# The final threshold search of an attention and expert kernel: comparisons against key differences, a written plan of fill-in work, and constants made ahead

## The chip, the cores and the metric

The kernel runs on one NeuronCore of one Trainium2 chip. The metric is device time in microseconds (us): the whole program once, from start to end; the median of several runs counts.

The engines have short names below. PE is TensorE (matrix products), PEld its weight loads, DVE is VectorE, ACT is ScalarE, POOL is GpSimd, SP is SyncE, which issues most DMA transfers. Each engine works its own instructions strictly in the order in which the program issues them.

## The reference

```
x = attention(q, kv, w_sr):                      # 4 batches, 12288 queries, 128 channels
    k = v = mean4x4(kv) @ w_sr                   # 768 keys and values per batch
    s = (q @ k.T) / sqrt(128)
    a = exp(s - max(s)); a /= sum(a) + 1e-9
    x = a @ v
for each batch b:                                # capacity = 128
    scores = x[b] @ w_gate                       # one score per row, 12288 of them
    top = the 128 rows with the largest score
    ye = relu(x[b, top] @ w1) @ w2               # w1 128x1024, w2 1024x128
    out[b] = x[b]; out[b, top] += sigmoid(scores[top]) * ye
```

## The kernel before

The work is cut into 192 blocks of 256 queries, 48 for each of the four batches, run in one loop (`for i in range(nb)`, nb = 192). One turn of the loop takes scores of block i+1 (`S`, PE into one of two PSUM buffers `s_buf`, shown as tiles `s`), the row maximum of block i (`s_max`, DVE), its exponentials (`exp`, ACT), their split in two 16-bit halves and transposes by DMA (`turn`, SP), and, `LAG` = 5 turns later, the product with the values (`AV`, 2 x 18 matmuls on PE into the PSUM tile `o_two`). From that product DVE takes the reciprocal `rz` of the row sum (`sums`, `recip`), the gate score of each row (tile `sc`) and the scaled output rows (`finish`, tile `x`); every fourth block SP stores an `x` tile of 512 KB. The tile `x` has two buffers.

Each batch then needs its 128 best rows. For batches 0 to 2 this (`topk`, `pick`) is a generator, kept in the list `select`, of which the loop takes one piece per turn; it is advanced by `advance(select)`. Its last piece of the third batch, the expert product of the 128 rows it picked (gather of the rows into `xe`, `xt`, the products with `w1` into `hs`, with `w2`, and a scatter into `out`) is still open when the loop ends.

After the loop comes the tail, which this change rewrites. Five blocks, 187 to 191 (`tail`), still lack their product, and the last batch its search:

1. Gate scores of the last two blocks are not taken from their products but from the exponentials, four DVE instructions of 768 columns into `kv_sum` (`gsum`).
2. `AV` of blocks 187 to 189, 30 filler matmuls (`warm`, products of ones that nobody reads), then `put` for each: scores and, on ACT because `ended` is set, the scaled rows `x`. `key_part` turns scores into sortable integers (`key`), whose upper 16 bits are `high` and lower 16 `low`.
3. `find` searches the 16-bit threshold digit by digit, two bits at a time, eight steps; it runs once on `high`, then on `rest` (the low halves of those that tie). In a step three thresholds are tested: DVE compares the 96 columns with a threshold and sums the hits (`junk`, `cnt3`), for two thresholds or three; where ACT is free it takes the third with a sign function (a "shared" step). PE sums the counts over the partitions with a matrix of ones into `counts` (tile `s`), DVE compares these with the need (`hit`, its sum is `dig`), and makes the next thresholds `tv` from `dig` and `base3`.
4. In every step `fill()` issues one piece of other work: in the first three a piece of `select`, then a piece of `later()` (half of an `AV` of 18 matmuls, or a `put` of blocks 190 and 191) and beside it a piece of `select` as long as that is not one for PE; when `later` is done, `select` alone.
5. `pick` makes row numbers from the threshold, gathers the rows (`xe`), runs what is left of `select`, 12 filler matmuls, then the expert product of the last batch and its scatter, the last transfer of the program.

The step in `fill` and the start of a step in the chain of `find` read, before:

```
if len(steps) > 3 and next(rows, True) is None:
    if select and select[0][1] != "pe":
        advance(select)
else:
    advance(select)
...
dve.scalar_tensor_tensor(out=tv, in0=dig.broadcast_to([P, 3]), scalar=float(1 << sh), in1=base3, op0=ALU.mult, op1=ALU.add)
```

Every engine call goes through one helper, so that all rows of the profile carry its line, L54; the tile names tell the instructions apart.

Of the kernel before, what the change touches and what calls it, by code (L numbers as in the profile page):

```python
# [19 lines left out]
P = 128  # L20
# [48 lines left out]
def attention_topk_mlp(ctx, tc, a, outs, capacity):  # L69
# [432 lines left out]
    def sums(n):  # L502
        b, blk = blocks[n]
        o, sg = st[n]["o"], kvset[b]["sg"]
        rz = sm.tile([P, QT], F32, name="rz")
        r = dve.tensor_scalar(out=rz, in0=o[:, :, C], scalar1=1e-9, scalar2=sg[:, 3:4], op0=ALU.add, op1=ALU.mult)
        st[n]["rz"] = rz
        st[n]["reads"] = [r.ins]
# [6 lines left out]

    def finish(n):
        b, blk = blocks[n]
        o, rz = st[n]["o"], st[n]["rz"]
        if blk % GROUP == 0:
            xt_[b] = ob.tile([P, GROUP * QT, C], F32, name="x")  # L520
        x = xt_[b]
        if b not in scores:
            scores[b] = tk.tile([P, NCOL], F32, name="sc")
        rows = x[:, (blk % GROUP) * QT:(blk % GROUP + 1) * QT]
        r = []
        if not direct(n):
            r.append(dve.tensor_tensor(out=scores[b][:, blk * QT:(blk + 1) * QT], in0=o[:, :, C + 1], in1=rz, op=ALU.mult))
        if ended:
            r += scaled(rows, o, rz)
        else:  # L530
            r.append(dve.tensor_tensor(out=rows, in0=o[:, :, 0:C], in1=rz.rearrange("p (j o) -> p j o", o=1).broadcast_to([P, QT, C]), op=ALU.mult))
# [5 lines left out]
        st[n].setdefault("reads", []).extend(y.ins for y in r)  # L537
# [53 lines left out]
    def pick(b, mask):  # L591
# [32 lines left out]
        for j0 in range(0, capacity, P):  # L624
# [125 lines left out]
    spare = [s_buf[i][:, 2 * k:2 * k + 2].rearrange("p k q -> p (k q)")[:, 0:QT * VC].rearrange("p (j c) -> p j c", j=QT) for i, k in ((0, 0), (1, 1), (1, 2))]  # L750
    gates = s_flat[0][:, BANK:BANK + M]
    tail = list(range(nb - LAG, nb))
    dest = dict(zip(tail, (spare[0], o_all, spare[1], spare[2], o_all)))
    whole = sm.tile([P, 2 * QT], F32, name="whole")

    def search_constants():
        jt = tk.tile([P, 3], F32, name="jt")
        for j in range(3):
            pool.memset(jt[:, j:j + 1], float(j + 1))
        half16 = tk.tile([P, P], BF16, name="half16")  # L760
        pool.memset(half16, -0.5)
        mid16 = tk.tile([P, 1], BF16, name="mid16")
        pool.memset(mid16, NCOL / 2.0)
        tv0 = tk.tile([P, 3], F32, name="tv0")
        dve.tensor_scalar(out=tv0, in0=jt, scalar1=float(1 << 14), scalar2=-0.5, op0=ALU.mult, op1=ALU.add)
        return jt, half16, mid16, tv0

    for i in range(nb):
# [4 lines left out]
        if i == nb - NBLK // 2:  # L773
            jt, half16, mid16, tv0 = search_constants()
# [6 lines left out]
        if i == nb - 1:  # L781
            room["select"] = lot
        s_max(i)
        if old:
            AV(m, 0)
# [40 lines left out]
        if i == nb - 1:  # L826
            for k in range(KT):
                pe.transpose(gates[:, k * P:(k + 1) * P], kvset[b]["raw"][:, k, 2 * P:].broadcast_to([P, P]), ident)
            AV(tail[0], 0, spare[0])
# [7 lines left out]
        if i == nb - 1:  # L837
            AV(tail[0], 1, spare[0])
        if old:
            sums(m)  # L840
            recip(m)
            finish(m)
# [24 lines left out]
    sc = scores[b]  # L867
    key = tk.tile([P, NCOL], I32, name="key")
    high, low, eqh, rest = (tk.tile([P, NCOL], U16, name=x) for x in ("high", "low", "eqh", "rest16"))
    junk = tk.tile([P, 3, NCOL], BF16, name="junk16")  # L870

    def put(m):
        if not direct(m):
            sums(m)
            recip(m)
        finish(m)
        return st[m]["reads"]

    def key_part(lo, hi):
        k, x = key[:, lo:hi], sc[:, lo:hi].bitcast(I32)  # L880
        dve.tensor_scalar(out=k, in0=x, scalar1=31, scalar2=-(1 << 31), op0=ALU.arith_shift_right, op1=ALU.bitwise_or)
        dve.tensor_tensor(out=k, in0=k, in1=x, op=ALU.bitwise_xor)
        dve.tensor_copy(high[:, lo:hi], k.bitcast(U16).rearrange("p (n h) -> p n h", h=2)[:, :, 1])

    part = kvu.tile([P, P, TAPS // 2], F32, name="kv_sum").rearrange("p k t -> p (k t)")[:, 0:M]
    gsum = sm.tile([P, 2 * QT], F32, name="gsum")
    for k in range(2 * QT):
        r = dve.scalar_tensor_tensor(out=part, in0=st[nb - 2 + k // QT]["a"][:, k % QT * M:(k % QT + 1) * M], scalar=1.0, in1=gates, op0=ALU.mult, op1=ALU.mult, accum_out=gsum[:, k:k + 1])
        others(r, st[tail[0]]["av"])
# [3 lines left out]
    dve.tensor_tensor(out=sc[:, NCOL - 2 * QT:], in0=gsum, in1=share, op=ALU.mult)  # L893
# [3 lines left out]
    for m in tail[1:3]:  # L897
        for j in range(QT):
            AV(m, j, dest[m])
    warm(30, s_flat[1][:, 0:P])  # L900
    put(tail[0])
    put(tail[1])
    key_part(0, NCOL - 3 * QT)
    put(tail[2])
    key_part(NCOL - 3 * QT, NCOL)

    def later():
        for m in tail[3:]:
# [3 lines left out]
            put(m)  # L912

    rows = later()
    steps = []
# [11 lines left out]
    def find(x, need, name, then=None):  # L927
        tv = tv0
        lo = tk.tile([P, 1], F32, name=name)
        pool.memset(lo, -0.5)  # L930
        shared = True
        for sh in range(14, -1, -2):
            cnt = tk.tile([P, 3], BF16, name="cnt3")
            n = 2 if shared else 3
            if shared:
                with nc.allow_low_precision(reason="whole numbers up to 96"):
                    act.activation(junk[:, 2], x, AF.Sign, bias=tv[:, 2:3], scale=-1.0, accum_out=cnt[:, 2:3])
                pe.matmul(counts[:, 2:3], ones16, mid16, start=True, stop=False)
                pe.matmul(counts[:, 2:3], half16, cnt[:, 2:3], start=False, stop=True)
            for j in range(n):  # L940
                dve.tensor_scalar(out=junk[:, j], in0=x, scalar1=tv[:, j:j + 1], scalar2=None, op0=ALU.is_ge, op1=ALU.add, accum_out=cnt[:, j:j + 1])
            if sh < 14:
                dve.scalar_tensor_tensor(out=lo, in0=dig, scalar=float(1 << sh + 2), in1=lo, op0=ALU.mult, op1=ALU.add)
            pe.matmul(counts[:, 0:n], ones16, cnt[:, 0:n], start=True, stop=True)
            base3 = tk.tile([P, 3], F32, name="base3")
            if sh:
                dve.tensor_scalar(out=base3, in0=jt, scalar1=float(1 << (sh - 2)), scalar2=lo, op0=ALU.mult, op1=ALU.add)
            else:
                dve.tensor_scalar(out=base3[:, 0:1], in0=lo, scalar1=0.5, scalar2=None, op0=ALU.add)
# [6 lines left out]
            dig = tk.tile([P, 1], F32, name="dig")  # L956
            hit = tk.tile([P, 3], F32, name="hit")
            dve.tensor_scalar(out=hit, in0=counts[:, 0:3], scalar1=need, scalar2=None, op0=ALU.is_ge, op1=ALU.add, accum_out=dig)
            if sh:
                tv = tk.tile([P, 3], F32, name="tv")  # L960
                dve.scalar_tensor_tensor(out=tv, in0=dig.broadcast_to([P, 3]), scalar=float(1 << sh), in1=base3, op0=ALU.mult, op1=ALU.add)
# [50 lines left out]
```

## Time and profile before

| | |
|---|---|
| median of 3 runs | 959.62 us (954.93 to 960.31) |
| the profiled execution's own time | 958.85 us |
| its span, first to last instruction | 957.1 us |
| PE busy | 899.7 us (94%) |
| PE weight loads busy | 725.8 us (76%) |
| DVE busy | 701.9 us (73%) |
| ACT busy | 753.6 us (79%) |
| POOL busy | 737.5 us (77%) |
| mean granted clock of TensorE | 0.979 |

The busy shares are means over a long loop in which PE is nearly always at work and a tail of some 60 us in which no engine is. What a change in the tail is worth is read from the tail's own rows: the timeline lists the instructions in order of time with the idle time ahead of each and what ended it.

### The profile page before, as it was taken

How to read it: one execution, taken by the hardware profiler on the slowest of the kernel's cores; microseconds unless marked ns; L12 is line 12 of the kernel's file. 1: busy time of each engine (PE TensorE's matmuls, PEld its weight loads, DVE VectorE, ACT ScalarE, POOL GpSimd, SP SyncE). 2: the span in 40 equal slices, each digit the busy share in tenths (PEclk: the TensorE clock that was granted, in tenths of full speed). 3: DMA queues.
4: the chain of work that ended last, by engine and by line, in shares of the span. 5: the costliest groups of instructions: out<-in, count | busy, mean ns of one | idle time of the engine just before them, and what ended most of it. 6: DMA issues, size and time to landing. Idle time of an engine off the chain costs nothing. (4 is left out here: it accounts for less than half of the span.)

```text
span 957.1 us, 26028 instructions
## 1 busy us (share of the span) xinstructions
PE 899.7 (94%) x10163; PEld 725.8 (76%) x10163; DVE 701.9 (73%) x1873; ACT 753.6 (79%) x1234; POOL 737.5 (77%) x496
## 2 busy tenths in 40 slices
PE   4899999999999999999999999999999998999946
PEld 3677888777877777877788787777788786788745
DVE  6666767667767776877667787777767886888873
ACT  2888888888978876888978787788988986889631
POOL 2789989888888887988888898889777776777601
PEclk9999999999999999999999999999999999999957
DMA  9899999999999999999999999999999999999910
GB/s 359 217 192 229 239 214 226 218 213 238 232 224 242 236 218 224 215 237 212 237 220 212 238 220 224 229 242 237 215 230 226 230 232 223 220 231 226 208 73 9
DMA packets 545084, 209.80 MB, mean 219 GB/s; under 512 B 524992, under 2 KB 526528, under 8 KB 544576
## 3 DMA queue, kind: packets, MB, share of 16 engines
q1 hardware_dynamic: 544704, 207.61, 108.0%
q8 instruction: 79, 1.29, 0.6%
q0 software_dynamic: 256, 0.52, 0.2%
q14 instruction: 45, 0.37, 0.1%
HBM read 52.04 MB, written 25.43 MB: 81 GB/s over the span
## 5 line engine op out<-in xcount | busy, mean ns | idle before, releaser
L54 POOL TENSOR_TENSOR hl<-am,hl 128x1280 bf16<-128x1280 f32 x192 | 499.5, 2602 | 151.8 <-ACT hl L54 105.6
L54 PEld LDWEIGHTS <-at 128*128 128x128 f16 (+1 forms) x6912 | 401.0, 97 | 64.8 <-issue 48.5
L54 PE MATMUL o_two<-vx,at 128*128 128x130 f16 x6804 | 435.6, 220 | 12.3 <-DMA at<-hl 10.5
L54 ACT ACTIVATE am<-s,m 128x512 f32<-128x512 f32 (+1 forms) x528 | 358.3, 706 | 36.8 <-DVE m L54 29.9
L54 DVE TENSOR_REDUCE m<-s 128x2 f32<-128x1536 f32 x191 | 335.5, 1757 | 50.2 <-PE s L54 50.2
L54 PE MATMUL s<-kh,qh 128*128 128x256 f32 (+1 forms) x771 | 363.5, 474 | 0.0
L54 ACT CAST hl<-am 128x1280 f16<-128x1280 f32 x192 | 240.4, 1252 | 26.6 <-DMA at<-hl 13.8
L54 PE MATMUL s<-kl,qh 128*128 128x256 bf16 (+1 forms) x771 | 256.2, 332 | 4.3 <-DVE hl L54 3.5
L54 PE MATMUL s<-kb,ql 128*128 128x256 bf16 (+1 forms) x771 | 251.4, 326 | 1.6 <-POOL ql L54 0.6
L54 PEld LDWEIGHTS s<-kh,qh 128*128 128x128 f32 x771 | 147.0, 191 | 48.6 <-issue 0.6
L54 DVE TENSOR_TENSOR at<-s,at 128x256 bf16<-128x256 f32 (+1 forms) x167 | 67.8, 406 | 94.2 <-ACT at L54 94.0
L54 POOL TENSOR_TENSOR ql<-q_raw,qh 128x512 bf16<-128x512 f32 x96 | 122.6, 1277 | 11.8 <-ACT qh L54 11.8
L54 PEld LDWEIGHTS <-qh 128*128 128x128 bf16 x771 | 75.2, 98 | 58.7 <-issue 49.5
L54 ACT CAST at<-s 128x256 f16<-128x256 f32 (+1 forms) x167 | 59.7, 357 | 69.5 <-PE s L54 69.3
L54 PEld LDWEIGHTS <-ql 128*128 128x128 bf16 x771 | 76.3, 99 | 11.7 <-POOL ql L54 5.5
L54 DVE TENSOR_TENSOR x<-o_two,rz 128x256 f32<-128x256 f32 x187 | 77.6, 415 | 0.0
L54 DVE TENSOR_SCALAR rz<-o_two,sg 128x2 f32<-128x2 f32 x188 | 40.9, 217 | 38.4 <-PE o_two L54 37.5
L54 PE MATMUL s<-cst,am 128*128 128x128 f32 x311 | 62.3, 276 | 3.3 <-ACT am L54 3.1
L54 ACT CAST qh<-q_raw 128x512 fp32r<-128x512 f32 x96 | 59.5, 620 | 7.0 <-DMA q_raw<-in_q 6.9
L54 POOL TENSOR_TENSOR kv_sum<-kv_raw 128x256 f32<-128x256 f32 x72 | 52.9, 734 | 0.0
L54 PEld LDWEIGHTS s<-cst,am 128*128 128x128 f32 x311 | 36.4, 140 | 6.6 <-ACT am L54 5.8
L54 PEld LDWEIGHTS <-ones 128*128 128x128 bf16 x334 | 27.0, 106 | 14.6 <-issue 14.2
(198 smaller groups left out, 547.4 us busy)
## 6 DMA issues: line engine op xcount, KB each, us to landing
out<-x SPq DMA_DIRECT2D x48, 512.0 KB, 3.7
q_raw<-in_q SPq DMA_DIRECT2D x46, 512.0 KB, 4.9
kv_raw<-in_kv SPq DMA_DIRECT2D x39, 512.0 KB, 5.0
at<-hl SPq DMA_TRANSPOSE x384, 4.8
kv_raw<-in_kv SPq DMA_DIRECT2D x3, 1024.0 KB, 9.4
q_raw<-in_kv SPq DMA_DIRECT2D x2, 512.0 KB
w<-in_w SPq DMA_DIRECT2D x2, 512.0 KB, 8.0
q_raw<-in_q SPq DMA_DIRECT2D x1, 768.0 KB
```

Source lines behind the costliest of these rows:

```text
L54: r = f(*args, **kwargs)
```

## The change

The change touches the last turn of the loop and the tail; nothing ahead of it differs but where constants are made.

- `search_constants` (five POOL fills at one place, one DVE instruction) becomes a list of 22 POOL fills, one per turn of the loop from block 168 on.
- In the last turn, DVE makes the keys of the first 84 of 96 columns ahead of the row maximum, PE makes the transposed gate weights (`gates`) ahead of `AV` of block 186, and two of the four 768-column sums run there. The other two stand between the score instructions of blocks 186, 187 and 188.
- The scaled rows of blocks 186 to 189 move to ACT (block 186 from DVE); those of blocks 188 and 189 are no longer made ahead of the search but in its first two steps. The last `x` tile (blocks 188 to 191) uses a free buffer of the pool for `kv_raw` in place of one of the two `x` buffers.
- The 30 filler matmuls ahead of the search are gone; the filler ahead of the last expert product grows from 12 to 36, and comes right after the gather, since all of `select` is done ahead of `pick`.
- `fill` follows a written plan: "r" is a piece of rows (`later`), "s" one of `select`, in each step up to two of them, PE work of `select` included. The products of blocks 190 and 191 use other PSUM places (`dest`).
- In a step of `find` the sum of hits is weighted by the digit's place (`powers`), `digs`, and a test compares `x - base >= digs` in one instruction, with `digs` spread over the columns as a second tensor; `tv` and `lo` are gone, `near` (the next base) is new and stands between the first and the second test. On ACT a shared test takes two instructions: `ahead` (the negated difference, made a step ahead) and the sign with `digs` as its bias.

```
+        if i >= nb - NBLK // 2 and constants:
+            pool.memset(*constants.pop(0))
...
+                xt_[b] = kvp.tile([P, 2, P // 2, TAPS], F32, name="kv_raw").rearrange("p h k t -> p (h k t)")[:, 0:GROUP * QT * C].rearrange("p (g c) -> p g c", c=C)
...
-                while select:
-                    advance(select)
-                warm(12, s_buf[0][:, KT - 1, 0:P])
+                warm(36, s_buf[0][:, KT - 1, 0:P])
...
-    warm(30, s_flat[1][:, 0:P])
...
+    plan = ["rs", "rs", "rs", "rs", "r", "rs", "rs", "ss", "rs", "s", "rs", "r"]
 
     def fill():
-        steps.append(True)
-        if len(steps) > 3 and next(rows, True) is None:
-            if select and select[0][1] != "pe":
-                advance(select)
-        else:
-            advance(select)
+        for c in plan.pop(0) if plan else "rs":
+            if c == "r":
+                next(rows, None)
+            else:
+                advance(select)
...
+            def test(j):
+                if digs is None:
+                    dve.tensor_scalar(out=junk[:, j], in0=x, scalar1=base[:, j + 1:j + 2], scalar2=None, op0=ALU.is_ge, op1=ALU.add, accum_out=cnt[:, j:j + 1])
+                else:
+                    dve.scalar_tensor_tensor(out=junk[:, j], in0=x, scalar=base[:, j + 1:j + 2], in1=digs.broadcast_to([P, NCOL]), op0=ALU.subtract, op1=ALU.is_ge, accum_out=cnt[:, j:j + 1])
...
+            test(0)
+            if digs is not None:
+                near = tk.tile([P, 4], F32, name="near")
+                dve.tensor_scalar(out=near, in0=pre, scalar1=digs, scalar2=None, op0=ALU.add)
+                pre = near
...
+            if shared and sh:
+                act.activation(ahead, x, AF.Identity, bias=base[:, 3:4], scale=-1.0)
...
+            dve.scalar_tensor_tensor(out=hit, in0=counts[:, 0:3], scalar=need, in1=powers[:, sh // 2], op0=ALU.is_ge, op1=ALU.mult, accum_out=digs)
...
+    for _ in rows:
+        pass
+    while select:
+        advance(select)
```

How the instructions stand on three engines. First ACT, from the copy of the last shares (`whole`) into the first steps of the search on `high`; before:

```order
L54 COPY whole<-s_113 128x4
L54 ACTIVATE x<-s_113,rz 128x128 x2
L54 ACTIVATE x<-o_two,rz 128x128 x2
L54 ACTIVATE x<-s_114,rz 128x128 x2
L54 ACTIVATE junk_15230,cnt_15371<-high,tv_13355 128x96
L54 ACTIVATE junk_15230,cnt_15390<-high,tv 128x96
```
and with the change, from the rows of block 186 on:

```order
L54 ACTIVATE x<-o_two,rz 128x128 x2
L54 ACTIVATE x<-s_113,rz 128x128 x2
L54 COPY whole<-s_113 128x4
L54 ACTIVATE junk_15254,cnt_15354<-high,start_303 128x96
L54 ACTIVATE kv_raw<-s_114,rz 128x128 x4
L54 ACTIVATE ahead<-high,near 128x96
L54 ACTIVATE junk_15254,cnt_15410<-ahead,digs 128x96
```
The rows of blocks 188 and 189, which stood ahead of the first sign test, now stand behind it, and go to a `kv_raw` buffer.

Second DVE, one step of the search on `high` (s_113 holds the counts); before, from the end of one step to the end of the next:

```order
L54 TENSOR_SCALAR base_15476<-jt,th_15369 128x3
L54 TENSOR_SCALAR hit,dig<-s_113 128x3
L54 SCALAR_TENSOR_TENSOR tv<-dig,base_15476 128x3
L54 TENSOR_SCALAR junk_15230,cnt_15492<-high,tv 128x96 x2
L54 SCALAR_TENSOR_TENSOR th_15369<-dig,th_15369 128x1
L54 TENSOR_SCALAR base_15500<-jt,th_15369 128x3
L54 TENSOR_SCALAR hit,dig<-s_113 128x3
```
and with the change, from the sum of one step to that of the next:

```order
L54 SCALAR_TENSOR_TENSOR hit,digs<-s_113,powers 128x3
L54 SCALAR_TENSOR_TENSOR junk_15254,cnt_15410<-high,near,digs 128x96
L54 TENSOR_SCALAR near<-pre,digs 128x4
L54 SCALAR_TENSOR_TENSOR junk_15254,cnt_15410<-high,near,digs 128x96
L54 TENSOR_SCALAR pre<-jt,near 128x4
L54 SCALAR_TENSOR_TENSOR hit,digs<-s_113,powers 128x3
```
`tv`, which lay between the sum and the first test, and the update of `th` are gone; `near` stands between the two tests.

Third PE; before, the expert product of the third batch stands at the end of `pick`, behind the products with the one-hot rows `oh`:

```order
L54 LDWEIGHTS oh
L54 MATMUL s_114<-pay,oh 128x2
L54 LDWEIGHTS oh
L54 MATMUL s_114<-pay,oh 128x1
L54 MATMUL lot<-xt,w_117 128x128 x4
L54 MATMUL lot<-w_118,hs 128x128 x8
L54 LDWEIGHTS ones_110
L54 MATMUL s_113<-ones_110 128x128
```
and with the change its first half stands in the last step of the search on `high`, ahead of the count of those above the threshold:

```order
L54 MATMUL s_113<-cnt_15501,ones_110 128x3
L54 MATMUL lot<-xt,w_117 128x128 x4
L54 LDWEIGHTS ones_110
L54 MATMUL s_113<-above,ones_110 128x1
L54 LDWEIGHTS ones_110
L54 MATMUL s_113<-mid_307,ones_110 128x1
L54 LDWEIGHTS half_306
L54 MATMUL s_113<-cnt_15530,half_306 128x1
```
The products with `w` moved from behind the search into it, where the counts of the search stand behind them in PE's order.

## Rows read from the trace of the kernel before

**Rows 1.** The page, its head line.

```profile
span 957.1 us, 26028 instructions
```
**Rows 2.** Timeline, 896 to 910 us: start us, us, engine, line, instruction.

```profile
896.62 1.76 DVE L54 TENSOR_REDUCE m<-s 128x2 f32<-128x1536 f32 x1 [1.09 <-PE s L54]
...
903.27 2.21 PE L54 MATMUL s<-vx,at 128*128 128x130 f16 x36
...
907.20 0.22 DVE L54 TENSOR_SCALAR rz<-s,sg 128x2 f32<-128x2 f32 x1 [0.68 <-PE s L54]
...
908.46 0.31 DVE L54 TENSOR_SCALAR_CACHE_REDUCE junk<-high,tv 128x96 bf16<-128x96 uint16 x1
...
908.93 0.22 DVE L54 TENSOR_SCALAR base<-jt,th 128x3 f32<-128x3 f32 x1
...
909.06 0.20 DVE L54 COPY low<-key 128x96 uint16<-128x96 uint16 x1
```
**Rows 3.** Timeline, 911 to 914 us, the first step's end.

```profile
911.58 0.62 ACT L54 ACTIVATE x<-o_two,rz 128x128 f32<-128x128 f32 x2 [5.70 <-DMA out<-x]
...
913.45 0.16 DVE L54 TENSOR_SCALAR_CACHE_REDUCE hit<-s 128x3 f32<-128x3 f32 x1 [4.12 <-PE s L54]
```
**Rows 4.** Timeline, 919 to 922 us, one shared step on high.

```profile
919.93 0.16 DVE L54 TENSOR_SCALAR_CACHE_REDUCE hit<-s 128x3 f32<-128x3 f32 x1
...
920.21 0.16 DVE L54 SCALAR_TENSOR_TENSOR tv<-dig,base 128x3 f32<-128x3 f32 x1
...
920.40 0.31 DVE L54 TENSOR_SCALAR_CACHE_REDUCE junk<-high,tv 128x96 bf16<-128x96 uint16 x1
...
920.64 0.31 DVE L54 TENSOR_SCALAR_CACHE_REDUCE junk<-high,tv 128x96 bf16<-128x96 uint16 x1
...
921.06 1.14 PE L54 MATMUL s<-vx,at 128*128 128x130 f16 x9
...
921.24 0.16 DVE L54 TENSOR_SCALAR_CACHE_REDUCE hit<-s 128x3 f32<-128x3 f32 x1
```
**Rows 5.** Timeline, 922 to 925 us, between the two searches.

```profile
922.55 0.16 DVE L54 TENSOR_SCALAR_CACHE_REDUCE hit<-s 128x3 f32<-128x3 f32 x1
...
923.32 0.16 PE L54 MATMUL s<-above,ones 128*128 128x1 bf16 x1
...
923.80 0.31 DVE L54 TENSOR_SCALAR_CACHE_REDUCE junk<-rest,tv 128x96 bf16<-128x96 uint16 x1
...
924.61 0.22 DVE L54 TENSOR_SCALAR_CACHE_REDUCE hit<-s,need 128x3 f32<-128x3 f32 x1
```
**Rows 6.** Timeline, 931 to 941 us, second search's end and pick.

```profile
931.77 0.29 DVE L54 SCALAR_TENSOR_TENSOR gw<-xe,cst 128x128 f32<-128x128 f32 x1
...
933.31 2.05 PE L54 MATMUL lot<-xt,w 128*128 128x128 f32 x8
...
935.50 0.22 DVE L54 TENSOR_SCALAR_CACHE_REDUCE hit<-s,need 128x3 f32<-128x3 f32 x1 [0.74 <-PE s L54]
...
938.91 0.29 PE L54 MATMUL s<-pay,oh 96*128 96x2 bf16 x4
...
940.34 0.96 POOL L54 DMA_INDIRECT xe<-out,idx  x1 [29.63 <-DVE g L54]
```
**Rows 7.** DMA view, 938 to 958 us: issue, count, us to landing.

```profile
xe<-out,idx POOLq DMA_INDIRECT x1, 2.5
```
**Rows 8.** Timeline, 941 to 948 us, PE ahead of the last product.

```profile
941.81 3.78 PE L54 MATMUL lot<-w,hs 128*128 128x128 f32 x16 [0.69 <-ACT hs L54]
...
945.38 1.49 PE L54 MATMUL s<-ones 128*128 128x128 bf16 x12
...
946.66 0.42 PE L54 MATMUL s<-cst,xe 128*128 128x128 f32 x1
...
947.47 2.05 PE L54 MATMUL s<-xt,w 128*128 128x128 f32 x16 [0.39 <-DVE xt L54]
```
**Rows 9.** One-us window: length, busy us (count) by engine, PEclk, DMA, GB/s.

```profile
946.00:947.00 1.00, 1.00 (x10) 0.79 (x7) 0.00 (x0) 0.00 (x0) 0.65 (x2) 0.52 0.00 0
```

More of the change, by code (lines that the diff above doesn't have):

```diff
@@ L514, in scaled, with gate_scores @@
         return [act.activation(rows[:, j], o[:, j, 0:C], AF.Copy, scale=rz[:, j:j + 1]) for j in range(QT)]
+    def gate_scores(n):
+        b, blk = blocks[n]
+        if b not in scores:
+            scores[b] = tk.tile([P, NCOL], F32, name="sc")
+        dve.tensor_tensor(out=scores[b][:, blk * QT:(blk + 1) * QT], in0=st[n]["o"][:, :, C + 1], in1=st[n]["rz"], op=ALU.mult)
     def finish(n):
@@ L754, in attention_topk_mlp @@
+    gsum = sm.tile([P, 2 * QT], F32, name="gsum")
     whole = sm.tile([P, 2 * QT], F32, name="whole")
[L756 to L766, printed above, removed]
+    jt, start0, next0 = (tk.tile([P, 4], F32, name=x) for x in ("jt", "start0", "next0"))
@@ L768, in attention_topk_mlp, with gate_sum @@
+    def gate_sum(n, j):
+        k = (n - nb + 2) * QT + j
+        r = dve.scalar_tensor_tensor(out=part, in0=st[n]["a"][:, j * M:(j + 1) * M], scalar=1.0, in1=gates, op0=ALU.mult, op1=ALU.mult, accum_out=gsum[:, k:k + 1])
+        others(r, st[tail[0]].get("av", ()))
     for i in range(nb):
@@ L782, in attention_topk_mlp @@
             room["select"] = lot
+            key = tk.tile([P, NCOL], I32, name="key")
+            high = tk.tile([P, NCOL], U16, name="high")
+            part = kvu.tile([P, P, TAPS // 2], F32, name="kv_sum").rearrange("p k t -> p (k t)")[:, 0:M]
+            done = NCOL - QT * (LAG + 1)
+            key_part(0, done)
         s_max(i)
+        if i == nb - 1:
+            for k in range(KT):
+                pe.transpose(gates[:, k * P:(k + 1) * P], kvset[b]["raw"][:, k, 2 * P:].broadcast_to([P, P]), ident)
         if old:
@@ L838, in attention_topk_mlp @@
             AV(tail[0], 1, spare[0])
+        if i == nb - 1:
+            for j in range(QT):
+                gate_sum(i - 1, 1 - j)
         if old:
@@ L866, in attention_topk_mlp @@
     b = blocks[n][0]
-    sc = scores[b]
-    key = tk.tile([P, NCOL], I32, name="key")
-    high, low, eqh, rest = (tk.tile([P, NCOL], U16, name=x) for x in ("high", "low", "eqh", "rest16"))
+    low, eqh, rest = (tk.tile([P, NCOL], U16, name=x) for x in ("low", "eqh", "rest16"))
     junk = tk.tile([P, 3, NCOL], BF16, name="junk16")
+    ahead = tk.tile([P, NCOL], F32, name="ahead")
     def put(m):
[L873 to L889, printed above, removed]
+        sums(m)
+        recip(m)
+        gate_scores(m)
+    for m in tail[1:3]:
+        for j in range(QT):
+            AV(m, j, dest[m])
+    finish(tail[0] - 1)
+    gate_sum(n, 1)
+    put(tail[0])
+    finish(tail[0])
+    gate_sum(n, 0)
     share = s_flat[0][:, 300:300 + 2 * QT]
@@ L911, in later, with find @@
                     yield
-            put(m)
+            finish(m)
+            yield
     rows = later()
-    steps = []
+    plan = ["rs", "rs", "rs", "rs", "r", "rs", "rs", "ss", "rs", "s", "rs", "r"]
     def fill():
-        steps.append(True)
-        if len(steps) > 3 and next(rows, True) is None:
-            if select and select[0][1] != "pe":
+        for c in plan.pop(0) if plan else "rs":
+            if c == "r":
+                next(rows, None)
+            else:
                 advance(select)
-        else:
-            advance(select)
     counts = s_buf[0][:, 0, 0:4]
[L927 to L930, printed above, removed]
+    def find(x, need, then=None):
+        base, pre, digs = start0, next0, None
         shared = True
```

94 lines of the change are left out of this document (48 added, 46 removed).

## The prediction

> **What bounds the kernel now.** I read the page first. Its 40 slices show PE at work almost all the time up to the last two or three, so the loop is not what the edits touch; the span is 957.1 us [rows 1] and the profiled execution's own time 958.85 us, 1.75 us more. Then the chain of waits from 895 us on. It leaves PE near 903 us and runs from there over one store, the DVE steps of the two searches, the products of the third batch on PE, and the last gather, product and scatter. Then the timeline of that stretch, piece by piece. The reader is to see five things.
>
> First, the start of the search is late twice. The last score instruction waits 0.68 us for PE until 907.20 although the product it reads ends at 903.27 + 2.21 = 905.48; in PE's order the 30 filler matmuls lie between. And the first step's tests start at 908.46 [rows 2], but its `hit` only at 913.45, after 4.12 us of idle DVE, because ACT, which owes it a sign test, sat 5.70 us in front of a row scaling that needs the `x` buffer of a store not yet landed [rows 3].
>
> Second, a shared step takes 921.24 - 919.93 = 1.31 us and is a chain on DVE: `hit`, `tv` 0.28 later, the first test 0.19 after `tv`, the second 0.24 later, and the next `hit` 0.60 after that, PE's count between [rows 4].
>
> Third, PE work that stands in front of a count stalls a step: the first half of the product with `w1`, eight matmuls of fp32 halves, took 2.05 us and its step's `hit` waited 0.74 us [rows 6].
>
> Fourth, the last gather starts 4.84 us after the last `hit` (940.34 against 935.50) and lands 2.5 us later [rows 6, 7], at 942.84; the transposition of its rows starts at 946.66 [rows 8]. PE was busy with the rest of the third batch and fillers for 3.8 us after the data were there.
>
> Fifth, PE's granted clock, of its levels 1.2 and 2.4 GHz, is at the lower one there until late. It rose to 2.4 GHz at about 946.96 (0.52 in that window, so 4% of it at full) [rows 9], 5.15 us after PE had started the products with `w2` at 941.81 [rows 8].
>
> **The change, part by part.** The sum is of differences against the 957.1 us of the profiled execution.
>
> *Start of the search.* PE's work up to the product of block 189 is the same in amount; only the gate transposes come ahead of block 186. Without fillers the last score can start at 905.5 and not 907.20: -1.7 us. DVE must be ready by then: its list is the old one less 84 columns of keys and less one row scaling. The keys moved ahead of the row maximum stand in 1.09 us of idle DVE [rows 2]; they are three short instructions like `base` and `low` (0.22 and 0.20 [rows 2]), some 0.7 us. Without that cover they would cost those 0.7 us. I put 0 for them.
>
> *First step.* With the last `x` tile in a buffer that no store holds, and the rows of blocks 188 and 189 behind the sign test, ACT is free. The first step of the second search shows an undisturbed one: test at 923.80, `hit` at 924.61, 0.81 us [rows 5]. Here it carries `pre`, `low` and the row numbers `idx` too, so 0.88. Before it was 913.45 - 908.46 = 4.99: -4.1 us. The upper bound, if ACT still waits for something, is 0.
>
> *The steps.* Removed: `tv` and the wait for it, 0.19. Added between the tests: `near`, a small instruction that waits for nothing new. The nearest row is `low` starting 0.13 after `base` [rows 2]; its upper bound is the 0.28 of an instruction that does wait. So -0.06 to +0.09 a step; I take -0.06, since `near` waits for nothing. `th` and `base` stood behind the tests, where PE's count hid them as it now hides `pre`. A test itself becomes another instruction with a second tensor. The nearest rows are the old test at 0.31 and `gw`, the same instruction form with a sum, 0.29 for 128 columns [rows 4, 6]: I take no difference; the range is 0 to +0.1 (below). On ACT the sign no longer waits for `tv`, and the extra `ahead` is done a step ahead; I put 0 for both, hidden beside DVE's tests.
>
> In the search on `high` three of seven steps are now without ACT, because the plan puts its row scalings there, and make a third test on DVE at 0.24 each [rows 4]: 7 x -0.06 + 3 x 0.24 + 0.15 for a transposition ahead of a count = +0.45, put at +0.4 us. In the second search three steps are unshared as before; there 7 x -0.06 = -0.4, and -0.2 for `gw`, which moves to a place where PE's count hides it. The second half of `w1` stalls a step as its first half did. A new stall is where half a product (nine matmuls, 1.14 us [rows 4]) and a quarter of `w2` (3.78 / 4 = 0.95 us [rows 8]) stand in one step of about 1.3 us: +0.7. Sum +0.1.
>
> *Between the searches.* The first half of `w1` now stands right behind the last count of the first search. The count of those above the threshold came 0.77 us after the `hit` (923.32 against 922.55) [rows 5]; it will wait for 2.05 us of products that start about 0.2 us ahead of the `hit`, so up to 1.1 us later, and DVE's `need`, with all tests of the next search queued behind it, waits too. The row of the same product delayed a `hit` by 0.74. I take 0.9; at full clock it would be 0.
>
> *End.* All of `select` is gone from between the gather and the last product. The one-hot products ended at 938.91 + 0.29 = 939.20, 3.7 us after the last `hit`; 36 fillers at the rate of the twelve (1.49 / 12 = 0.124 us each [rows 8]) end 8.2 us after it. The gather lands 4.84 + 2.5 = 7.3 us after it, so the fillers bind. Before it was 946.66 - 935.50 = 11.2: -3.0 us, and between -1.4 (a gather of twice 2.5 us) and -3.9 (gather bound, the clock up early).
>
> *The last product.* Before, the products with `w1` ran at full clock, 2.05 us for sixteen against 2.05 us for eight at half [rows 6, 8], and `w2` likewise. Those now follow 36 fillers without the long run of work ahead. PE is dense from about 3.1 us after the `hit`; with the rise 5.15 us later that is 8.2 us, and the product starts 0.8 us after its transposition, at 9.0. So 0; the bound is both products at half clock, +4.1 us.
>
> Constants: 22 short POOL fills in turns where POOL is not last: 0.
>
> Sum: -1.7 - 4.1 + 0.4 + 0.1 + 0.9 - 3.0 + 0 = -7.4 us. The span becomes 949.7, its execution 951.45 us. The median of the runs shown, 959.62, is 0.8 above the profiled execution, and by it the result is 952.2. I predict 951.8, between the two.
>
> **The rivals.**
>
> *The new test is slow* (the one that ends on the other side). On the path lie 34 tests of the new form, 17 in each search. If the spread `digs` as a second tensor costs p more per test, the result is -7.4 + 34 p: nothing is gained from p = 0.22, and over 0.36 us the kernel is slower by more than 0.5%. At p = 0.4 it is -7.4 + 13.6 = +6.2, 965.8 by the median. Against it stands `gw`, with two fp32 tensors from SBUF and a sum: 128 columns in 0.29 us, less than the old test's 0.31 for 96. No row has a 16-bit tensor beside a spread one. The Trainium skill, "Vector Engine (DVE) Microarchitecture Reference", section "Points that are easy to get wrong", says that this form with two sources that are not bf16 in SBUF runs at half throughput; that speaks against the new test and not against the old. By it each test would take about 0.1 us longer, an estimate of mine from that page, and the time would be near 955.6. By its 0.29 us for `gw` the trace disagrees. Worked from rows, a test that takes its 0.31 us and a third more, p = 0.1, gives -7.4 + 3.4 = -4.0 us, 955.6 by the median: within 0.5%.
>
> *The last product at half clock.* If the rise does not come within the fillers and the gap behind them, w1 and w2 cost up to 4.1 us: -3.3, 956.3. For it: the burst of 2.05 us at 933.31 left the clock where it was, for `w2` still took 3.78 us for its sixteen [rows 6, 8]. Against it: 4.5 us of unbroken fillers.
>
> *PE wins its clock inside the search.* Products, `w1` and `w2` stand so close there that the clock may rise earlier; then the stalls of 0.9 and 0.7 and the second half of `w1` (0.7) vanish: -9.7, 949.9 by the median and lower by the profiled execution.
>
> *The store's stall stays*, because ACT or PE waits for something else in the first steps (the gather for the third batch, half a product): up to 4.1 is lost, 956.3.
>
> **How the numbers follow.** 0.5%, 4.8 us, is about what a measurement of this kernel can tell from no change. Forecast 0.62 (950 to 954.5), clock early 0.11 (down to 948.5), product at half clock 0.10, tests a third dearer 0.07, stall stays 0.06, tests far dearer 0.04. Faster by over 0.5%: the first two and a little of the others, 0.76; within: 0.20; slower: 0.04. The range leaves out 2 in 10: 948.6 to 956.3.
>
> **What would show it.** Right: ACT's first sign test starts with DVE's, at about 906.8 us; the first `hit` near 907.7; shared steps of 1.24 us; the last `hit` near 931; the last transposition about 8 us behind it at full clock soon after. Wrong: tests with a duration well over 0.31 us, an ACT wait for a store, `hit` idle for PE in many steps, or a PEclk of 0.5 in the windows of the last product.

## The result, and the profile after

The changed kernel took a median of 944.83 us in its first six executions (939.13 to 952.71), against 958.9 for the kernel before beside it: a ratio of 0.986, with a 95% interval of 0.981 to 0.991, or 13.1 us (8.4 to 17.8). The ratios here and below leave out executions more than 1.5% above the fastest of their kernel. The forecast was 951.8, with a range of 948.6 to 956.3. The sign was right and the forecast gain too small.

The head line of the page after, against [rows 1]:

```profile
span 940.4 us, 25828 instructions
```

The span fell by 16.7 us. To see where, I took the start of every row maximum (`m`, one per block) in both traces, and the same marks in the tail.

| stretch | before | after | difference |
|---|---|---|---|
| start to the row maximum of block 167 (instructions nearly the same) | 790.15 | 784.33 | -5.8 |
| block 167 to 170 (the constants of before) | 17.65 | 12.62 | -5.0 |
| block 170 to 191 | 88.82 | 89.69 | +0.9 |
| last row maximum to the end | 60.48 | 53.76 | -6.7 |

The tail gave 6.7 us, near the 7.4 of the forecast. The other 10 us lie in the loop, where the forecast had nothing. The first row of the table lies within the loop's scatter: from block 1 to 167, twelve profiles of the changed kernel and its variants below took 754.7 to 767.0 us, on the mean 761.3, and the kernel before 762.3. First the tail. Timeline after, from the last products to the first `hit` (start us, us, engine, line, instruction, idle time and what ended it), to be read beside [rows 2, 3]:

```profile
895.13 1.55 PE L54 MATMUL s<-vx,at 128*128 128x130 f16 x24 [1.02 <-DMA at<-hl]
...
896.72 0.22 DVE L54 TENSOR_SCALAR rz<-s,sg 128x2 f32<-128x2 f32 x1 [1.80 <-PE s L54]
...
898.50 0.31 DVE L54 TENSOR_SCALAR_CACHE_REDUCE junk<-high,start 128x96 bf16<-128x96 uint16 x1
...
898.87 1.12 ACT L54 ACTIVATE kv_raw<-s,rz 128x128 f32<-128x128 f32 x4
...
899.38 0.16 DVE L54 SCALAR_TENSOR_TENSOR hit<-s,powers 128x3 f32<-128x3 f32 x1
```

ACT scales its rows behind the first sign test without a wait for a store, and the first `hit` comes 0.88 us after the first test. But the last score still comes late: PE now waits for the last transposes by DMA ahead of its last product. In the search, a shared step and the two halves of the product with `w1`, beside [rows 4 to 6]:

```profile
902.20 0.16 DVE L54 SCALAR_TENSOR_TENSOR hit<-s,powers 128x3 f32<-128x3 f32 x1
...
902.41 0.32 DVE L54 SCALAR_TENSOR_TENSOR junk<-high,near,digs 128x96 bf16<-128x96 uint16 x1
...
902.65 0.22 DVE L54 TENSOR_SCALAR near<-pre,digs 128x4 f32<-128x4 f32 x1
902.78 0.31 DVE L54 SCALAR_TENSOR_TENSOR junk<-high,near,digs 128x96 bf16<-128x96 uint16 x1
...
903.36 0.16 DVE L54 SCALAR_TENSOR_TENSOR hit<-s,powers 128x3 f32<-128x3 f32 x1
...
904.60 0.16 DVE L54 SCALAR_TENSOR_TENSOR hit<-s,powers 128x3 f32<-128x3 f32 x1 [0.19 <-ACT ahead L54]
...
908.29 1.14 PE L54 MATMUL lot<-xt,w 128*128 128x128 f32 x8
909.29 0.16 PE L54 MATMUL s<-above,ones 128*128 128x1 bf16 x1
...
911.79 2.05 PE L54 MATMUL lot<-xt,w 128*128 128x128 f32 x8
...
913.99 0.22 DVE L54 SCALAR_TENSOR_TENSOR hit<-s,need,powers 128x3 f32<-128x3 f32 x1 [0.91 <-PE s L54]
```

The step (the fourth) takes 903.36 - 902.20 = 1.16 us, the three after it 1.23 or 1.24. In two of these `hit` waits for ACT's `ahead`, an instruction that the prediction put at nothing. The first half of `w1` ran at full clock and delayed nothing; the second, at half clock, held up a `hit` by 0.91 us. The end, beside [rows 6 to 8]:

```profile
920.63 0.22 DVE L54 SCALAR_TENSOR_TENSOR hit<-s,need,powers 128x3 f32<-128x3 f32 x1
...
924.31 4.00 PE L54 MATMUL s<-ones 128*128 128x128 bf16 x36
...
925.58 0.97 POOL L54 DMA_INDIRECT xe<-out,idx  x1 [2.23 <-DVE idx L54]
...
928.28 0.45 PE L54 MATMUL s<-cst,xe 128*128 128x128 f32 x1
...
929.11 3.79 PE L54 MATMUL s<-xt,w 128*128 128x128 f32 x16 [0.38 <-DVE xt L54]
...
933.68 2.05 PE L54 MATMUL s<-w,hs 128*128 128x128 f32 x16 [0.78 <-DVE g L54]
```

From the last `hit` to the transposition it is 7.65 us (11.16 before). The product with `w1` then ran at half clock, 3.79 us for the 2.05 of before; that with `w2` was at full clock again.

Now the loop. The one place where it lost time before and no longer does is block 168. The timeline of the kernel before there:

```profile
795.89 2.37 POOL L54 TENSOR_TENSOR hl<-am,hl 128x1152 bf16<-128x1152 f32 x1 [1.76 <-ACT hl L54]
...
798.20 0.17 POOL L54 MEMSET jt<- 128x1 f32 x3
...
798.40 0.17 DVE L54 TENSOR_SCALAR tv<-jt 128x3 f32<-128x3 f32 x1 [4.43 <-POOL jt L54]
...
798.48 1.75 DVE L54 TENSOR_REDUCE m<-s 128x2 f32<-128x1536 f32 x1
...
800.61 0.37 PE L54 MATMUL s<-kl,qh 128*128 128x256 bf16 x1 [3.49 <-DVE hl L54]
```

`search_constants` put five short fills on POOL, and behind them one DVE instruction that reads `jt`. The fills stood behind POOL's long `hl`, DVE waited 4.43 us for them, and in DVE's order the row maximum of block 168 stood behind the wait. ACT waited for that maximum, and PE 3.49 us for `hl`, the DVE instruction behind it. The two blocks took 13.27 us in place of 8.40. Not all of that is the wait: the row maximum of block 168 came 8.33 us after that of block 167, in place of 4.24, and PE's granted clock was at 0.50 from 800.6 to 803.2 us, which delayed the next one. The change leaves no DVE reader there, and the same row maximum starts with 0.43 us of idle time:

```profile
788.57 1.76 DVE L54 TENSOR_REDUCE m<-s 128x2 f32<-128x1536 f32 x1 [0.43 <-PE s L54]
```

### The profile page after: what moved, and what is told of

The parts are those of the page before. It is cut to its first block, busy times and chain, and to the rows that moved or that the text cites. A ratio compares the mean times of both kernels' runs of the same rounds, so it can differ in the third digit from the quotient of the medians.

```text
span 940.4 us, 25828 instructions
## 1 busy us (share of the span) xinstructions
PE 892.3 (95%) x9969; PEld 725.0 (77%) x10151; DVE 700.2 (74%) x1861; ACT 756.4 (80%) x1238; POOL 738.2 (78%) x511
## 4 chain that ended last, share of the span: by engine, by line
PE 66%; DMA 12%; POOL 8%; issue 7%; DVE 3%; ACT 3%; SPq 0%; POOLq 0%; ACTq 0%; DVEq 0%
PE s L54 35%; PE o_two L54 31%; DMA at<-hl 11%; POOL hl L54 3%; POOL kv_sum L54 3%; POOL ql L54 2%; ACT hl L54 1%; ACT am L54 1%; DMA kv_raw<-in_kv 1%; DVE junk L54 1%; SPq L54 0%; DVE m L54 0%; PE lot L54 0%; ACT at L54 0%; DMA xe<-out,idx 0%
## 5 line engine op out<-in xcount | busy, mean ns | idle before, releaser
L54 PE MATMUL s<-kl,qh 128*128 128x256 bf16 (+1 forms) x697 | 227.1, 326 | 1.2 <-DVE pm L54 0.9
L54 PE MATMUL s<-kb,ql 128*128 128x256 bf16 (+1 forms) x663 | 209.7, 316 | 5.6 <-POOL ql L54 0.9
L54 POOL TENSOR_TENSOR ql<-q_raw,qh 128x512 bf16<-128x512 f32 x96 | 122.6, 1277 | 11.7 <-ACT qh L54 11.6
L54 DVE RECIPROCAL rz<-rz 128x2 f32<-128x2 f32 x190 | 31.5, 166 | 6.5
```

The lines of the kernel that those rows point to most:

```text
L54: r = f(*args, **kwargs)
```

## The experiments

The executions of one kernel scatter by some 4 us (standard deviation), so stages are read from the traces and totals only from many runs. "Changed" is the kernel after the change. Its first profile is the one above; the second and the third come from the two unaltered reruns below. Ratios are against the kernel before on the same chip.

**The constants: one alone, one undone, four of them.** Before, with the fills spread and the first thresholds made by fills:

```
-            jt, half16, mid16, tv0 = search_constants()
+        if i >= nb - NBLK // 2 and constants:
+            pool.memset(*constants.pop(0))
```

> The kernel before with one edit: its constants are made one POOL fill per turn from block 168 on, the first thresholds by fills too, so that no DVE instruction reads a fresh fill. Theory (the constants held up the loop once): DVE's wait of 4.43 us at block 168 is gone, the two turns around it fall from 13.3 us to 8.4, and the time falls by 4.4 to 4.9 us. Rival (PE had that time in hand, as the prediction put it at nothing): the turn recovers later in the loop, and the time is the same within 1 us.

The wait is gone, and the two blocks take 8.40 us. The time is 957.81 against 957.86, ratio 0.998 (0.994 to 1.002): 1.9 us less, between 6.0 less and 2.2 more. That excludes neither the theory nor the rival.

Changed, with fills and DVE readers of them back at block 168 (one of the two readers is shown):

```
+        for j in range(4):
+            pool.memset(jt[:, j:j + 1], float(j))
...
+        dve.tensor_scalar(out=start0, in0=jt, scalar1=float(1 << 14), scalar2=-0.5, op0=ALU.mult, op1=ALU.add)
```

> The changed kernel with the reverse edit: six POOL fills at block 168 and two DVE instructions that read them, as before; the other fills stay spread. Theory (the constants held up the loop once): two turns near block 168 take 4 to 5 us longer than their neighbours and the time rises by 4.4 to 4.9 us over that of the changed kernel beside it. Rival (worth nothing): the same within 1 us.

Its timeline at block 168:

```profile
791.62 0.17 DVE L54 TENSOR_SCALAR start<-jt 128x4 f32<-128x4 f32 x1 [4.47 <-POOL jt L54]
...
793.91 0.27 PE L54 MATMUL s<-kl,qh 128*128 128x256 bf16 x1 [3.60 <-DVE hl L54]
```

The wait is back. The two blocks take 12.13 us; behind the wait PE's granted clock was 1.00 here (793.9 to 796.5 us), not 0.50 as before. The ratio is 0.9955 (0.992 to 0.999), against 0.990 (0.984 to 0.996) for changed on the same chip: 5.3 us more, as the theory has it, but the two intervals overlap. What is shown is the wait at its place, not its price in the total.

Changed, with four such waits:

```
+        if i in (60, 96, 132, 168):
+            pool.memset(fresh[:, k:k + 1], 1.0)
+            dve.tensor_scalar(out=copied[:, k:k + 1], in0=fresh[:, k:k + 1], scalar1=2.0, scalar2=None, op0=ALU.mult)
```

> The changed kernel with one POOL fill and one DVE instruction that reads it, as they stood ahead of block 168 before, at blocks 60, 96, 132 and 168. Theory (each such wait holds the row maximum behind it, and the loop gets nothing back): each costs the 4.1 to 4.9 us that it cost at block 168, so 16 to 19 us over the changed kernel beside it. Rival (the transposes by DMA run behind and catch up while PE stands still, so that later waits for them go): PE's waits for transposes fall in the profile and the time rises by less, 6 to 13 us. Second rival (one wait costs nothing in the end): 0 to 3 us.

Its four waits on the timeline, and the view of PE's waits from 60 to 905 us (total us, times, longest) for before, changed and this kernel:

```profile
298.80 0.15 DVE L54 TENSOR_SCALAR copied<-fresh 128x1 f32<-128x1 f32 x1 [5.68 <-POOL fresh L54]
468.59 0.15 DVE L54 TENSOR_SCALAR copied<-fresh 128x1 f32<-128x1 f32 x1 [4.40 <-POOL fresh L54]
639.80 0.15 DVE L54 TENSOR_SCALAR copied<-fresh 128x1 f32<-128x1 f32 x1 [5.08 <-POOL fresh L54]
804.97 0.15 DVE L54 TENSOR_SCALAR copied<-fresh 128x1 f32<-128x1 f32 x1 [4.37 <-POOL fresh L54]
```
```profile
PE o_two L54 <- DMA at<-hl: 10.5, 13, 2.3
```
```profile
PE o_two L54 <- DMA at<-hl: 6.3, 9, 2.1
```
```profile
PE o_two L54 <- DMA at<-hl: 3.5, 6, 0.8
```

The ratio is 1.000 (0.997 to 1.003); the changed kernel with its old fillers, on the same chip, had 0.990 (0.986 to 0.994, four executions). That is 10 us for four waits, 2.5 us each, give or take about 1.2, where DVE waited 4.4 to 5.7: the first rival. PE waits for transposes less than in any other profile. What is given back shows behind block 168 too. From block 170 to 191 the three kernels with a wait there took 88.82 to 88.84 us, and PE waited for no transpose in that stretch; twelve profiles without one (the last two runs below left out) took 88.82 to 95.34, on the mean 91.4, and two of them, in which PE waited for no transpose either, 88.82 and 88.84. So of the 5.0 us that the loop lost at block 168, some 2.5 came back.

**The first step: buffer and place.** Changed, with `x` from its old pool and the two `finish` calls ahead of the search:

```
-            if n < nb - GROUP:
...
+    finish(tail[1])
     put(tail[2])
+    finish(tail[2])
```

> The changed kernel with the last x tile back in its old pool of two buffers and the scaled rows of blocks 188 and 189 back ahead of the search. Theory (the first step was late because ACT sat in a row scaling for a store's buffer): ACT waits for the store again and the time from the first test to the first hit goes from 0.88 us to 3 to 5 us. Rival (the stall was of the old step, or of the fillers): it stays under 1.2 us. From the last row maximum to the end the changed kernel took 53.8 and 52.1 us; here 55 to 58 by the theory.

```profile
902.94 0.62 ACT L54 ACTIVATE x<-s,rz 128x128 f32<-128x128 f32 x2 [8.27 <-DMA out<-x]
```
```profile
903.60 0.22 DVE L54 TENSOR_SCALAR rz<-s,sg 128x2 f32<-128x2 f32 x1 [6.73 <-ACT x L54]
```

The stall is back, but not where I put it: DVE itself waits for ACT ahead of the first test, so the first test comes 18.67 us after the last row maximum, the first `hit` 0.81 after it, and the tail takes 60.3 us. The ratio is 0.998 (0.995 to 1.000). Then each alone, in one execution each:

> The changed kernel with only the buffer undone: the last x tile is one of two again, its rows of blocks 188 and 189 stay in the first two steps of the search. Theory (the buffer and the place are both needed): ACT sits in front of the rows of block 188 until the store of blocks 180 to 183 has read its buffer, some 4.5 us after the first test, and the first step that gives ACT a test (the fourth) comes 1 to 3 us late; the first hit stays 0.88 us after the first test. Rival (the place alone cures it): no step is over 1.5 us and the tail stays at 51.4 to 53.9 us.

```profile
915.60 1.14 ACT L54 ACTIVATE x<-s,rz 128x128 f32<-128x128 f32 x4 [5.09 <-DMA out<-x]
```

The fourth step took 4.04 us, 2.9 too many, and the tail 55.6.

> The changed kernel with only the place undone: the rows of blocks 188 and 189 are scaled ahead of the search again, into the new buffer that no store holds. Theory (it was the buffer): no wait for a store; from the last row maximum to the first hit 12.7 us becomes 13 to 14, as DVE waits for one pair of rows (0.6 to 0.7 us) in its order and the first sign for the other. Rival (the place alone is what counts): 16 to 19.5 us, as with both undone (19.48).

No store is waited for; 12.59 us to the first test and 0.81 to the `hit` make 13.40, the tail 52.4. So the buffer does it: the wait for the store comes with the old buffer in either place, and goes with the new one in either. The later place of the rows is worth some 0.7 us at the first `hit`.

**The steps.** Changed, with the body of `find` from before:

> The changed kernel with the steps of the search as before (hit, then the next thresholds, then plain tests); all the rest stays. Theory (the new step saves the 0.19 us between the sum and the first test, less what the extra instruction costs): a shared step takes 1.31 us in place of 1.24, 14 to 15 steps give 0.7 to 1.3 us, and the time rises by about 1 us. Rival (the new test with a second tensor is dearer, and eats the gain): no change or faster by up to 1 us. Second rival (the stalls of PE and ACT set the step): within 0.3 us.

Its fourth step, to be read beside 902.20 to 903.36 above:

```profile
906.82 0.16 DVE L54 TENSOR_SCALAR_CACHE_REDUCE hit<-s 128x3 f32<-128x3 f32 x1
...
907.02 0.16 DVE L54 SCALAR_TENSOR_TENSOR tv<-dig,base 128x3 f32<-128x3 f32 x1
...
907.22 0.31 DVE L54 TENSOR_SCALAR_CACHE_REDUCE junk<-high,tv 128x96 bf16<-128x96 uint16 x1
...
908.03 0.16 DVE L54 TENSOR_SCALAR_CACHE_REDUCE hit<-s 128x3 f32<-128x3 f32 x1
```

It took 1.21 us in place of 1.16. Of the 15 intervals between one `hit` and the next I leave out the last on `high` and the one between the searches, which differ most (1.64 against 1.40 and 2.70 against 2.05; the second by PE's clock). The other 13 took 18.69 us, and 17.82 with the new body in the second profile of changed: 0.067 us a step on the mean, from nothing (the fifth step, where the new `hit` waits for `ahead`) to 0.23. The theory holds for the sum, not for each step. The total (ratio 0.993, 0.990 to 0.997) can't add to it.

**The start, the plan.** Changed, with `warm(30, s_flat[1][:, 0:P])` back ahead of the search:

> The changed kernel with the 30 filler matmuls back ahead of the search. Theory (what bounds the last score is now the landing of the last transposed block, and the fillers would come behind it): from the last row maximum to the first test 11.9 us becomes 12.5 to 13.6, since the last score waits for the fillers as it did before. Rival (fillers stand in a gap and cost nothing, as the unchanged 11.9 us suggests): it stays between 10.6 and 12.0.

12.34 us to the first test, between the two. Its transposes came in time and DVE waited for the fillers; where they come in time without fillers (seven profiles, the third of changed among them) it is 10.66 or 10.67. So the fillers do cost 1.7 us, unless the transposes are late anyway. With fillers and transposes in time the kernel before took 11.84, half a microsecond less than here. In the new order the products of blocks 188 and 189 lie in one PSUM tile, and DVE starts the score of either only when PE has ended both (896.72 in the profile after, behind 1.80 us of idle time; the second score starts at 897.25); before, one block's score was left at that point (907.20 [rows 2]).

Changed, with the old rule in `fill`:

> The changed kernel with the old rule of fill-in work (select in three steps, then rows with those pieces of select that are not for PE). Theory (the plan bought the end: products of the third batch no longer stand behind the last hit): from the last hit to the last transposition 7.65 us becomes 10 to 12, the steps of the second search get 0.5 to 1 us shorter in sum, and the tail is 54.5 to 57 us in place of 51.4 to 53.9. Rival (the end came from the 36 fillers and the gather's place, the plan is worth nothing): 7.5 to 8.5 us from hit to transposition, a tail under 54.

```profile
939.29 3.78 PE L54 MATMUL lot<-w,hs 128*128 128x128 f32 x16 [0.69 <-ACT hs L54]
942.86 0.29 PE L54 MATMUL s<-ones,mask 128*96 128x1 bf16 x2
```

The whole product of the third batch now stands between the last `hit` and the mask's products: 16.3 us to the transposition, a tail of 58.4. That is the theory's direction and more than its size, since all that the rule leaves of `select` is now done ahead of `pick` and no longer in the gather's shadow. The ratio is 1.000 (0.996 to 1.004).

**The last product's clock.** Changed once more, unaltered:

> The changed kernel once more, as the measure beside which the others stand and for the spread of the loop. If the shorter loop of its first profile is part of the change, the start of the last row maximum (block 191) comes again near 886.6 us, 10 us ahead of the 896.6 of the kernel before; if half of that was chance, it comes at 888 to 893, as the constants alone explain 4.4 to 4.9 us. From that row maximum to the end of the span it takes 53.8 us again (within 1 us) by either theory.

Ratio 0.990 (0.984 to 0.996), tail 52.08, last row maximum at 892.12. The difference in the tail is in the last product, seen in the windows of the two profiles (length, busy us (count) by engine, PEclk, DMA, GB/s), changed first:

```profile
924.00:928.00 4.00, 4.00 (x42) 3.92 (x41) 0.70 (x5) 0.00 (x0) 0.97 (x1) 0.50 0.09 27
928.00:933.00 5.00, 4.51 (x20) 3.71 (x18) 1.26 (x5) 0.20 (x1) 0.00 (x0) 0.50 0.00 0
```
```profile
929.00:932.00 3.00, 2.59 (x27) 2.44 (x28) 1.29 (x7) 0.00 (x0) 0.83 (x1) 0.50 0.07 25
932.00:933.00 1.00, 1.00 (x17) 1.00 (x16) 0.00 (x0) 0.00 (x0) 0.14 (x1) 0.83 0.24 49
```

In the second the clock rose within the 36 fillers, and both products ran at full clock; in the first not before the end of `w1`. Two attempts to hold it up follow.

```
+    warm(30, filler)
...
+                warm(8, filler)
```

> The changed kernel with more filler matmuls where PE stands idle in the tail: 30 behind the last product ahead of the search, 8 in each step that has no other PE work, 12 ahead of the one-hot products. Theory (the tail's products run at half clock because PE was idle ahead of them): the granted clock stays near 1.0 through more of the tail, the last product with w1 takes 2.05 us in place of 3.79, the step with the second half of w1 falls from 2.02 to about 1.5, and the tail from the last row maximum on is 51 to 52 us in place of 52.1 to 53.8. Rival (the fillers stand ahead of counts and cost more than the clock gives): shared steps over 1.3 us, the tail 53 us or more.

```profile
902.31 0.95 DVE L54 SCALAR_TENSOR_TENSOR kv_sum<-am,s 128x768 f32<-128x768 f32 x1 [6.20 <-PE s L54]
...
909.72 0.16 DVE L54 SCALAR_TENSOR_TENSOR hit<-s,powers 128x3 f32<-128x3 f32 x1 [0.89 <-PE s L54]
```

The rival, and worse: `filler` lies in the PSUM tile that also holds the gates and the counts, and DVE's readers of that tile waited for the fillers. The tail took 60.2 us, the ratio is 0.996 (0.993 to 0.999).

```
+        if last:
+            warm(12, lot[:, 0:P])
```

> The changed kernel with 12 more filler matmuls in the 1.4 us in which PE waits for the one-hot rows, into a PSUM tile that nobody reads then. Theory (the granted clock falls 25 us after the first test because PE stands idle ahead of it; without that gap it stays up, or rises in time): the last product with w1 takes 2.05 us, from the transposition to the end 10.3 us as in the better profiles, the tail 50.5 to 52 us. Rival (the clock falls from idle time that came earlier, and rises at its own time): 12.1 us in some executions as before, tail up to 54. Either way the one-hot products start no more than 0.2 us later.

The one-hot products were not late, the last product ran at full clock, and the tail was 51.9. But the clock had fallen long ahead of it (it was low from 15 to 27 us after the first test), so these fillers are not shown to be why. Ratio 0.988 (0.983 to 0.993): no better than changed, as far as these runs can tell.

**The loop's scatter.** The stretch from block 1 to 167 was the same work in 14 profiles, and took 754.7 to 767.0 us, nearly in step with PE's wait for transposes (with all of that wait from 60 to 905 us: 6.2 us with 755.5, 6.3 with 756.6, 10.9 with 760.0, 12.3 with 765.2, 13.4 with 767.0; counted within the stretch alone the correlation over the 14 is 0.95).

> The changed kernel a third time, beside the two below. If the tail (7.7 us) and one wait at block 168 less what the loop gives back (2.5 us) are all of the change, it is 10 us under the kernel before in its runs on the same chip, ratio 0.989 to 0.990; if the first runs' 13 us were the change itself, 0.986 or less.

Ratio 0.983 (0.978 to 0.988), resting on the four shortest of its twelve executions; the medians of all differ by 7.9 us (948.07 against 956.0). The one speaks for the second reading, the other for neither, so this run does not decide between them. Tail 51.66.

> The changed kernel with the 512 KB stores of x issued from ACT and no longer from SP, whose queue carries the transposes. Theory (the loop's scatter is PE waiting for transposes that stand in SP's queue behind stores and loads): PE's waits for transposes, 6 to 15 us so far, fall under 4, the stretch from block 1 to block 167, 755 to 767 us so far, is 753 to 757, and the time falls by 3 to 8 us. Rival (the DMA engines themselves are full, whichever queue feeds them): waits and times as in the changed kernel within 2 us. Second rival (ACT, which waits for x at the store, comes late with its next work): slower by over 5 us.

> The changed kernel with the 512 KB loads of queries issued from ACT and no longer from SP. Theory (as for the stores): PE's waits for transposes fall under 4 us and the time by 3 to 8 us. Rival (the DMA engines are full): within 2 us of the changed kernel.

Both were slower: 1.014 (1.009 to 1.019) and 1.006 (1.002 to 1.010). PE's waits, for the stores (two lines) and then for the loads:

```profile
PE o_two L54 <- DMA at<-hl: 22.1, 26, 1.9
PE s L54 <- ACT am L54: 10.4, 11, 2.5
```
```profile
PE o_two L54 <- DMA at<-hl: 18.6, 18, 4.8
```

The theory and the first rival fail: PE waits longer for the transposes, which landed 5.0 us after their issue in the median, against 4.7 to 4.9 in all other profiles. For the stores the second rival came in part: 21 us slower than changed on the same chip by the medians (969.39 against 948.07), and PE's wait for ACT's exponentials (`am`) rose from 3.0 us in the third profile of changed to 10.4. For the loads that wait was 2.2. That the loop's scatter goes with PE's waits for transposes stands; what makes them late in one execution and not in the next stays open.

## Why the prediction was wrong

In the tail, the terms against the first profile of changed and the two others:

| term (us) | predicted | first profile | all three |
|---|---|---|---|
| start of the search | -1.7 | 0.0 | 0.0, +0.1, -1.2 |
| first step | -4.1 | -4.1 | -4.1 each |
| search on `high` | +0.4 | 0.0 | 0.0, 0.0, +0.1 |
| between the searches | +0.9 | 0.0 | 0.0, 0.0, +0.8 |
| second search | +0.1 | -0.8 | -0.8 each |
| end | -3.0 | -3.5 | -3.5 each |
| last product | 0 | +1.7 | +1.7, -0.1, -0.1 |
| sum | -7.4 | -6.7 | -6.7, -8.4, -8.8 |

**The step that failed** is "Constants: 22 short POOL fills in turns where POOL is not last: 0". It priced the fills that were added and not the DVE instruction that was removed. That instruction had stood ahead of a row maximum, with a wait of 4.43 us for POOL; I read no row of block 168 before I wrote the zero. It cost the loop 5.0 us where it stood (4.1 of wait, the rest at half clock behind it) and, less what came back, some 2.5.

With the tail's -8.0 on the mean of three profiles and these -2.5 the change is worth some 10.5 us. The medians of the three sets of runs say 14.1, 11.7 and 7.9 less than before. The first set, on which the forecast is measured, had the loop on its good side as well: of the 16.7 us between the two first profiles 5.8 lie ahead of block 167, in unchanged work. The range lay too high by the constants and took no account of that scatter. The constants alone do not carry the miss: with -2.5 in the sum the forecast is 949.3 and the same range reaches down to 946.1, still above the 944.83. What is left goes with the loop's scatter; nothing here shows it to be part of the change, so I call it chance.

That the tail of the first profile came within 0.7 us of its sum is luck too. Its terms missed by +1.7 (start), -0.4, -0.9, -0.9, -0.5 (end) and +1.7 (last product), which nearly cancel.

Point by point. **First step**: right in size, and the buffer is the cause (the three experiments). **Steps**: right on the mean, 0.067 us a step for 0.06; but `ahead`, put at nothing, delays a `hit` in some. **End**: right in sign and, in the first profile, in what binds: the fillers, at 0.111 us each for 0.124, so that the transposition came 7.65 us after the `hit` and not 8.2. In the two others it waited for the gather (0.68 and 0.38 us). **Start**: right that fillers cost 1.7 us; in two of three profiles the wait for the last transposes (1.02 us in the first) took their place, while in the trace of before PE did not wait for them in the tail. Even in the third, with the transposes in time, the gain was 1.2 and not 1.7, since two blocks' scores now stand behind PE's last product. **Between** and **last product**: mis-sized both ways by the clock, which is at either level at these places in one execution and the next. The bound of +4.1 was too wide: `w2` was at full clock each time. **Second search**: the stall of 0.7 for half a product beside a quarter of `w2` did not come, as that quarter ran at full clock (0.69 us); `w1`'s second half stalled as said.

Of the rivals, the dearer test is out: 0.31 to 0.32 us with the second tensor (0.35 in the first that has it), 0.31 without. The rule that I weighed from the Trainium skill ("Vector Engine (DVE) Microarchitecture Reference", "Points that are easy to get wrong"), half throughput for this form with two sources that are not bf16 in SBUF, would have made it about 0.1 us longer by my estimate; the trace disagrees. The store's stall did not stay. The last product at half clock came in part, in one profile of three.

## What to carry to other kernels

A line that "makes constants" is priced by who reads them and what stands behind the reader in its engine's order, not by the fills; look at the trace where it stands before writing a zero. A stall in a loop that a second resource nearly bounds is worth less than its length, because the other resource catches up meanwhile: here about half. Where executions scatter by more than the terms, compare marks inside the traces, and let several profiles stand for one.

## What I had not expected of the hardware

The same program meets the first half of its last product (`w1`) at 1.2 or at 2.4 GHz: with 36 fillers ahead of it, the granted clock rose within 3 us of the first filler in one execution (929.90, and 0.83 in the window from 932) and 9 us in another (924.31, and 0.82 in the window from 933). With the large stores or loads on ACT's queue in place of SP's, the transposes came later, not earlier: PE waited 22.1 and 18.6 us for them in all, and 3.5 to 15 in the profiles with all of them on SP's.
